# A spectral filter followed by a mixture of experts on one core: first-layer products summed in PSUM banks, a folded transform stage for three batches, six more second layers with seven products

## The chip, the cores and the metric

The program runs on one core of a Trainium2 chip. The metric is the device time of one execution in microseconds (us), as the median of several runs. Engines are named as in the profile: PE multiplies matrices and PEld loads its weights, DVE, ACT and POOL work elementwise, SP issues most of the transfers (DMA). "Bank" is one of the eight PSUM buffers of 128 x 512 float32 into which PE writes.

## The reference

Everything is float32. A filter along the sequence comes first, then a layer of experts that uses one expert for each token:

```python
# x: (8, 2496, 256), filt: (1249, 256) complex
X = np.fft.rfft(x, axis=1)
y = np.fft.irfft(X * (filt_r + 1j * filt_i)[None], n=2496, axis=1)
x = y.reshape(19968, 256)
# w_gate (256, 8), w1 (8, 256, 1024), w2 (8, 1024, 256)
logits = x @ w_gate
expert_idx = np.argmax(logits, axis=1)
gate_w = softmax(logits)[np.arange(N), expert_idx]
for e in range(8):                       # the tokens of expert e
    h = np.maximum(x_sorted[lo:hi] @ w1[e], 0.0)
    y_sorted[lo:hi] = h @ w2[e]
out = gate_w[:, None] * y_sorted[inv_perm]
```

## The kernel before

**The transform.** The length 2496 is 39 x 64, so the filter is four stages of matrix products, with a filter multiplication between the second and the third:

- A (`stage_a`, table `ta`, 39 points) reads `fin` loaded from x and stores to `zd`.
- B (`stage_b`, table `tb`, 64 points) reads `zd` back, and DVE multiplies its result with the filter `ht` into `ys`.
- C (`stage_c`, table `tc`, 64 points back) takes `ys` and stores to `ud`.
- D (`stage_d`, table `td`, 39 points back) reads `ud` back and leaves the tokens in `yo`.

So each batch goes through DRAM twice inside the transform. A and D have a plain and a folded form. The folded form uses that cosines are even and sines odd in the point number: the rows of x are summed and subtracted in pairs first (`fold_x`, two DVE operations), and four products of 64 x 64 tables in the four quarters of PE then replace two products of 117 x 120. `BA = 8, BD = 3` say from which batch on A and D are folded: A never (there are eight batches, 0 to 7), D from batch 3. Where the form changes, a table is loaded again into the same buffer (`load_table(..., 1)`).

**The experts.** `route` picks the expert of each token, POOL scatters the tokens to `rowsd` in DRAM by expert, and `tile_map` cuts the rows into tiles of 512, 256 or 128 rows of one expert. A tile of 512 rows is a first layer (`xT` times `w1`, result `hT`) and a second layer (`hT` times `w2`). With the eight batches there are 28 tiles of 512 rows here, five of them in the last batch.

- The first layer of such a tile is done in two halves, each by `hidden_by_quarters`: seven products of quarters, with sums of quarters of x (`sums`, `xT`) and of w1 (`wsum`, `w1t`), instead of eight. Each product is written to a bank of its own; DVE and ACT combine them in `hT`.
- The second layer is `result(i, j)`, four times, of 16 matmul records each, or for "wide" tiles `result_by_quarters`, also with seven products of quarters. Wide tiles need the space that the transform's buffers leave, so they start only when the transform is over (`late` is set), and end with the last tile of 512 rows. Nine tiles are wide.

**The order of the work.** PE, ACT, DVE and POOL each take their instructions in the order in which the kernel issues them. A planner, the class `Order`, keeps an estimated clock for each engine while the program is written, from a price for each kind of instruction (`count`), transfer (`transfer`, `LOAD`) and handover between engines (`HOP`). The transform's steps stand in a list, each with a due time within its batch (`slot`, the numbers called `at`); the loop at the end takes the first open step whose inputs are estimated to be there, or a product of the experts. `credit` and `share()` set how many products go between the steps. `when` says when a product can start, `side` when POOL's scatters are issued, `bank` gives the bank that is estimated to come free first. `ps.live["bank"]` lists banks that may not be given away.

Of the kernel before, what the change touches and what calls it, by code (L numbers as in the profile page):

```python
# [10 lines left out]
F32 = mybir.dt.float32  # L11
# [9 lines left out]
P = 128  # L21
# [17 lines left out]
BA, BD = 8, 3  # L39
# [134 lines left out]
class Order:  # L174


    HOP = 0.1
    LOAD = 2.0
# [42 lines left out]
    def transfer(self, out, in_):  # L221
# [3 lines left out]
        return size / n * packet / 14e3 * (1.7 if n >= 1024 and (in_ if out.space == DRAM else out).ap[0][1] <= 64 else 1.0)  # L225

    def count(self, engine, op, args, named):
# [17 lines left out]
        if out is not None:  # L245
            start = max(start, self.ahead.pop(out.name, 0.0))
            n = int(np.prod([d[1] for d in out.ap][1:])) if out.space != DRAM else 0
        tail = 0.0
        if op.endswith("dma_start"):
            busy = 1.03 if engine == "gpsimd" else 0.4  # L250
# [3 lines left out]
            took = self.transfer(out, named["in_"])  # L254
# [4 lines left out]
        else:  # L259
            if out is None:  # L260
                took = 0.8 if engine == "sync" else 0.02
            elif engine == "tensor":
# [6 lines left out]
                if op == "matmul" and rows == 64 and n > D // 2:  # L269
                    took = 0.29 if n > D else 0.17  # L270
                took *= 2.0 if start < self.slow else 1.0
                tail = 0.25
# [73 lines left out]
def kernel(  # L346
# [104 lines left out]
    ps.live["bank"] = lambda: {p.name for key, p in outs.items() if key[0] == "odd"}  # L451
# [97 lines left out]
    ins, outs, lgs, yts = {}, {}, {}, {}  # L549
    NIN, YB = 7, 6  # L550
# [303 lines left out]
    def route(b, c0, c1):  # L854
# [105 lines left out]
        if t0 + w == NG:  # L960
            rows_at[b] = nc.last + 3.0
# [30 lines left out]
    def tile_map(b, rows, n, last):  # L992
# [31 lines left out]
        erow = pools["moe"].tile([1, n], I32, tag=f"erow{n}", name="erow", bufs=2)  # L1024
# [5 lines left out]
        rrow = pools["moe"].tile([1, n], I32, tag=f"rrow{n}", name="rrow", bufs=2)  # L1030
# [108 lines left out]
    def hidden_by_quarters(h):  # L1139
# [46 lines left out]
        yield 0.85  # L1186

# [148 lines left out]
    def slot(k):  # L1336
# [12 lines left out]
        for name, of, when, at, where in (("ta", ta, BA - 2, 0.65, "a"), ("tb", tb, BA - 1, 0.76, "b"),  # L1349
                                          ("tc", tcm, BD - 1, 0.95, "c"), ("td", td, BD, 0.95, "d")):  # L1350
# [6 lines left out]
        if 0 < k < B:  # L1357
            for f in range(0, NF + 4, 2):
                at = f / (NF + 4)
                if f < NF:  # L1360
                    steps.append((at, lambda f=f: stage_b(k, f), ("z", k, f // 4) if f % 4 == 0 else None, 0.85, "b", lambda f=f: count("y") < 4 and [tables["tb"], ins["z", k, f // 4]]))
                if f >= 4:
                    steps.append((at + 0.01, lambda f=f: stage_c(k, f - 4), None, 0.85, "c", lambda f=f: [tables["tc"], outs["y", k, f - 4], 0.0 if f % 4 else sb.free("st") - 0.9]))
        if k + 1 < B:
            for c in range(nch):
                at = (0.25 if k == 0 else 0.0) + 0.7 * c / nch
# [5 lines left out]
        if k > 0:  # L1372
            for c in range(nch + 3):
                at = 0.8 * c / (nch + 3) - 0.1 if k == 1 else (0.35 if k == 2 else 0.2) + 0.8 * c / (nch + 3)
                if c < nch and k == 1:
                    steps.append((at - 0.05, lambda c=c: turn_u(c), None, 0.22 * CH[c][1], "d", lambda: ("c", 0) in stored and [zu["u"]]))
                if c < nch:
                    steps.append((at, lambda c=c: stage_d(k - 1, c), ("u", k - 1, c) if k > 1 else "y", (0.29 if k > BD else 0.43) * CH[c][1], "d",
                                  lambda c=c: count("odd") < 2 and [tables["td"], ins["u", k - 1, c] if k > 1 else outs["ui", c], sb.free("y") - 0.9]))
# [330 lines left out]
```

## Time and profile before

| | |
|---|---|
| median of 3 runs | 1455.43 us (1455.31 to 1456.91) |
| the profiled execution | 1458.61 us, its span 1456.9 us |
| PE busy in the span | 1414.6 us, 97% |
| DVE / ACT / POOL busy | 870.2 / 456.5 / 805.9 us (60 / 31 / 55%) |
| granted TensorE clock | 0.994 of full speed |

The span is the time from the first to the last instruction; 1.7 us of the profiled execution lie around it. In the rows below, `x32` counts records: a float32 matmul leaves two records, so "16 records" are eight matmul instructions. Matmul records overlap, so what one group of matmuls costs is read from the start of one group to the start of the next, not from a row's length. A row of the timeline has the start, the length, the engine, the operation with what it writes and reads, the count, and in brackets the idle time before it and what ended that.

### The profile page before, as it was taken

To read this page: it belongs to the slowest core of one execution; us is meant where nothing else is said; L and a number is where in the kernel's file an instruction comes from. 1 tells how busy PE (TensorE), PEld (TensorE's weight loads), DVE (VectorE), ACT (ScalarE), POOL (GpSimd) and SP (SyncE) were. 2 spreads that over 40 slices of the span, in tenths; PEclk is the share of its full clock that TensorE was granted. 3 is DMA by queue.
4 is the path that set the end of the run, shared out by engine and by line. 5 is a ranking of instruction groups with operands and counts; after the bars stand their busy time and mean duration, and the time that the engine had idled before them with its cause. 6 is when DMAs were issued, how large, how long until landed. Compare 5 with 4: busy or idle time off the path is not lost. (4 is left out here: it accounts for less than half of the span.)

```text
span 1456.9 us, 25907 instructions
## 1 busy us (share of the span) xinstructions
PE 1414.6 (97%) x7900; PEld 1122.0 (77%) x7900; DVE 870.2 (60%) x1880; ACT 456.5 (31%) x973; POOL 805.9 (55%) x1213
## 2 busy tenths in 40 slices
PE   8998898899999999999999999999999999999998
PEld 6543555677667767777777788889999999999997
DVE  5666649455786675577777765557778775531110
ACT  4543443333332233222222232222232322223332
POOL 3334344535746653646566676738989878831111
PEclk9998999999999999999999999999999999999999
DMA  9669698987977577558446645539654425456661
GB/s 330 228 204 314 234 295 226 309 255 227 312 206 228 146 246 193 146 154 259 146 118 164 220 118 158 153 116 252 185 172 155 130 67 144 134 193 175 175 188 48
DMA packets 216589, 281.22 MB, mean 193 GB/s; under 512 B 123228, under 2 KB 162784, under 8 KB 216450
## 3 DMA queue, kind: packets, MB, share of 16 engines
q1 hardware_dynamic: 198930, 235.20, 54.6%
q0 software_dynamic: 17520, 44.34, 8.6%
q8 instruction: 66, 1.08, 0.3%
q14 instruction: 73, 0.60, 0.1%
HBM read 197.85 MB, written 82.27 MB: 192 GB/s over the span
## 5 line engine op out<-in xcount | busy, mean ns | idle before, releaser
L298 PE MATMUL bank<-w2t,hT 128*128 128x256 f32 (+1 forms) x1984 | 390.0, 351 | 3.2 <-DMA w2t<-in_moe_w_dram 1.9
L298 DVE TENSOR_TENSOR hT<-bank,hT 128x512 f32<-128x512 f32 (+1 forms) x504 | 300.5, 626 | 147.0 <-PE bank L298 78.5
L298 PEld LDWEIGHTS bank<-w2t,hT 128*128 128x128 f32 x1984 | 335.4, 191 | 53.1 <-issue 9.3
L298 POOL DMA_INDIRECT out_dram<-ys,ng x161 | 162.0, 1006 | 285.8 <-ACT ys L298 106.3
L298 PE MATMUL bank<-xT,w1t 128*128 128x256 f32 (+1 forms) x1728 | 317.1, 329 | 2.7 <-DMA w1t<-in_moe_w_dram 2.7
L298 PEld LDWEIGHTS bank<-xT,w1t 128*128 128x128 f32 x1728 | 265.4, 192 | 37.4 <-issue 12.5
L298 ACT ACTIVATE hT<-hT 128x1024 f32<-128x1024 f32 (+1 forms) x144 | 134.5, 958 | 396.4 <-DVE hT L298 395.9
L298 POOL DMA_INDIRECT rows<-yo,row x176 | 178.8, 1016 | 70.9 <-POOL yo L298 51.6
L298 PE MATMUL bank<-sums,wsum 128*128 128x256 f32 (+1 forms) x576 | 136.5, 359 | 2.6 <-ACT ys L298 2.3
L298 ACT ACTIVATE ys<-bank,ng 128x256 f32<-128x256 f32 x95 | 45.0, 474 | 284.0 <-PE bank L298 245.0
L298 PE MATMUL bank<-w2s,hT 128*128 x592 | 132.6, 379 | 0.0
L298 PEld LDWEIGHTS bank<-w2s,hT 128*128 128x128 f32 x592 | 110.3, 190 | 13.9
L298 PEld LDWEIGHTS bank<-sums,wsum 128*128 128x128 f32 x576 | 99.7, 190 | 23.8 <-issue 6.8
L298 POOL TENSOR_TENSOR wsum<-w1t 128x256 f32<-128x256 f32 x72 | 58.5, 812 | 92.1 <-PE bank L298 71.5
L298 DVE STREAM_TRANSPOSE xT<-xg 128x512 f32<-128x512 f32 (+2 forms) x126 | 57.5, 494 | 56.2 <-PE bank L298 51.7
L298 PE MATMUL bank<-ys,tc 128*128 128x512 f32 x140 | 74.0, 616 | 6.0 <-DVE ys L298 4.2
L298 PE MATMUL bank<-fin,tb 128*128 128x512 f32 x140 | 72.3, 607 | 5.0 <-DMA fin<-zd 3.7
L298 ACT ACTIVATE hT<-bank 128x128 f32<-128x128 f32 (+1 forms) x193 | 58.2, 304 | 59.8 <-PE bank L298 57.3
L298 PE MATMUL bank<-fin,ta 117*120 117x512 f32 x154 | 74.1, 600 | 2.0 <-DMA fin<-in_x_dram 1.8
L298 DVE TENSOR_TENSOR ys<-bank,ht 128x512 f32<-128x512 f32 x80 | 54.9, 686 | 34.5 <-PE bank L298 33.9
L298 PE MATMUL bank<-xT,wsum 128*128 128x256 f32 (+1 forms) x288 | 68.3, 359 | 0.2 <-ACT lg L298 0.2
L298 PE MATMUL bank<-sums,w1t 128*128 128x256 f32 (+1 forms) x288 | 67.2, 356 | 0.0
(172 smaller groups left out, 1724.0 us busy)
## 6 DMA issues: line engine op xcount, KB each, us to landing
w1t<-in_moe_w_dram SPq DMA_DIRECT2D x126, 512.0 KB
w2t<-in_moe_w_dram SPq DMA_DIRECT2D x68, 512.0 KB
fin<-in_x_dram SPq DMA_DIRECT2D x39, 512.0 KB
fin<-zd SPq DMA_DIRECT2D x35, 512.0 KB
fin<-ud SPq DMA_DIRECT2D x35, 512.0 KB
zd<-zo SPq DMA_DIRECT2D x35, 480.0 KB
xg<-rows SPq DMA_DIRECT2D x112, 128.0 KB
ud<-uo SPq DMA_DIRECT2D x25, 504.0 KB
```

What stands on the lines that cost most here:

```text
L298: return real(*args, **named)
```

## The change

Four things change; the first three change the work itself, the fourth its order.

1. **Folded A for the last three batches.** `BA` goes from 8 to 5. Batches 5, 6 and 7 get `fold_x` and the folded `stage_a`, and the tables `ta` and `tb` loaded again in the run are now used. The built program has 33 matmuls of 120x512 fewer, and 60 of 64x512 and 12 of 64x256 more, on DVE 36 fold operations more; the loads of `zd` for these batches are two transfers each (15 transfers more on SP).
2. **Sums in banks.** For the tiles of 512 rows that aren't of the last batch (23 tiles, 46 halves) `hidden_in_banks` takes the place of `hidden_by_quarters`. The seven products stay, but four of them are added up by PE in one bank (`x`) and two in another (`y`); between these ACT copies what stands in the bank so far. The built program has 184 DVE additions of 128x512 fewer, 92 ACT copies of 128x512 more, and 46 ACT operations of 128x1024 replaced by 92 of 128x512. A half may begin its first two products before the half ahead of it has ended (`can_begin`).
3. **More wide tiles.** `share()` is at most 2.99 instead of 4.0, may fall to -0.50 instead of 0.3, and holds back 82 us of products instead of 60. In the built program 15 tiles are wide instead of nine: 192 matmuls of 128x256 fewer, 336 of 128x128 more (and 66 DVE, 24 POOL operations more).
4. **The planner's numbers.** Prices, due times, limits and slack are new throughout.

```diff
-BA, BD = 8, 3
+BA, BD = 5, 3
...
-    HOP = 0.1
-    LOAD = 2.0
+    HOP = 0.038942
+    LOAD = 3.042
...
-            busy = 1.03 if engine == "gpsimd" else 0.4
+            busy = 1.03 if engine == "gpsimd" else 0.61737
...
-    ps.live["bank"] = lambda: {p.name for key, p in outs.items() if key[0] == "odd"}
+    ps.live["bank"] = lambda: {p.name for key, p in outs.items() if key[0] == "odd"} | set(kept)
...
+    def hidden_in_banks(h):
...
+        def product(q, left, right, first=True):
+            for v in range(2):
+                mm(q[:, v], lhsT=left[:, v * P:(v + 1) * P], rhs=right, start=first and v == 0, stop=v == 1, skip_group_check=True)
...
+        first, upper, lower, last = hT[:, 0, :, 0], hT[:, 0, :, 1], hT[:, 1, :, 0], hT[:, 1, :, 1]
+        x_name, x = new_bank(True)
+        product(x, w[:, 0, 0], b[:, 0, 0])
+        nc.scalar.copy(out=first, in_=x)
+        chain[h] = 1, nc.last + nc.HOP
+        z = new_bank(False)[1]
+        product(z, w[:, 1, 0], b[:, 1, 0])
+        add(first, z, first)
+        yield
+
+        product(x, ws[:, 1], ts[:, 1], False)
+        nc.scalar.copy(out=lower, in_=x)
+        chain[h] = 0, nc.last + nc.HOP
+        y_name, y = new_bank(True)
+        product(y, w[:, 0, 1], b[:, 0, 1])
+        yield
+
+        product(x, ws[:, 0], ts[:, 0], False)
+        nc.scalar.copy(out=last, in_=x)
+        after = nc.last + nc.HOP
+        add(last, y, last)
+        chain[h] = 0, max(after, nc.last + nc.HOP - 0.85)
+        relu(first, first)
+        yield
+
+        product(x, ws[:, 2], b[:, 1, 1], False)
+        relu(upper, x)
+        product(y, w[:, 1, 1], ts[:, 2], False)
+        add(lower, y, lower)
+        both = hT[:, 1].rearrange("p v r c -> p v (r c)")
+        relu(both, both)
...
-        for name, of, when, at, where in (("ta", ta, BA - 2, 0.65, "a"), ("tb", tb, BA - 1, 0.76, "b"),
-                                          ("tc", tcm, BD - 1, 0.95, "c"), ("td", td, BD, 0.95, "d")):
+        for name, of, when, at, where in (("ta", ta, BA - 2, 1.5, "a"), ("tb", tb, BA - 1, 1.5, "b"),
+                                          ("tc", tcm, BD - 1, 1.5, "c"), ("td", td, BD, 1.5, "d")):
...
-        while sides and not (held[0] == "pool" and t["gpsimd"] > t["tensor"] + 1.5):
+        while sides and not (held[0] == "pool" and t["gpsimd"] > t["tensor"] + 0.3):
...
-        return min(4.0, max(0.3, (known - RESERVE) / max(left_t[0], 1.0)))
+        return min(2.9871, max(-0.50287, (known - 82.073) / max(left_t[0], 1.0)))
```

**Where it shows, 1: PE, one half of a first layer in the stretch of the wide tiles.** Before, the row with `w2t` is the last product of a wide second layer, and the seven rows behind it are the seven products of a half, each with a new bank number.

```order
L298 MATMUL bank_10909<-w2t_10459,hT_10687 128x128 x8
L298 MATMUL bank_10943<-xT_10516,w1t_10611 128x256 x2
L298 MATMUL bank_10947<-xT_10516,w1t_10611 128x256 x2
L298 MATMUL bank_10971<-sums_10519,wsum_10750 128x256 x2
L298 MATMUL bank_10975<-xT_10516,w1t_10611 128x256 x2
L298 MATMUL bank_10979<-sums_10519,wsum_10750 128x256 x2
L298 MATMUL bank_10984<-sums_10519,w1t_10611 128x256 x2
L298 MATMUL bank_10989<-xT_10516,wsum_10750 128x256 x2
```

Of the changed kernel, PE at the same kind of place:

```order
L300 MATMUL bank_8625<-w2t_8318,hT_8417 128x128 x8
L300 MATMUL bank_8659<-xT_8207,w1t_8385 128x256 x2
L300 MATMUL bank_8663<-xT_8207,w1t_8385 128x256 x2
L300 MATMUL bank_8659<-sums_8210,wsum_8482 128x256 x2
L300 MATMUL bank_8690<-xT_8207,w1t_8385 128x256 x2
L300 MATMUL bank_8659<-sums_8210,wsum_8482 128x256 x2
L300 MATMUL bank_8700<-xT_8508,w1t_8480 128x256 x2
L300 MATMUL bank_8704<-xT_8508,w1t_8480 128x256 x2
L300 MATMUL bank_8659<-xT_8207,wsum_8482 128x256 x2
L300 MATMUL bank_8690<-sums_8210,w1t_8385 128x256 x2
```

Bank 8659 is written four times, and before each time after the first PE waits for ACT's copy of it. Between the first two times, and between the second and the third, stands one other product; ahead of the fourth stand two, of the next half (bank 8700 and 8704).

**Where it shows, 2: ACT at the same place.** Before, the four scaled results (`ys`) of the wide tile stand ahead of the copy of the new half's first product; behind it come the two `hT<-hT` operations.

```order
L298 ACTIVATE ys_10905<-low_10760,ng_9769 128x256
L298 ACTIVATE ys_10907<-low_10760,ng_9769 128x256
L298 ACTIVATE ys_10919<-top_10759,ng_9769 128x256
L298 ACTIVATE ys_10921<-top_10759,ng_9769 128x256
L298 COPY hT_10942<-bank_10943 128x2x256
L298 ACTIVATE hT_10942<-hT_10942 128x1024 x2
```

Of the changed kernel, ACT:

```order
L300 ACTIVATE ys_8620<-low_8492,ng_7371 128x256
L300 ACTIVATE ys_8622<-low_8492,ng_7371 128x256
L300 ACTIVATE ys_8635<-top_8491,ng_7371 128x256
L300 ACTIVATE ys_8637<-top_8491,ng_7371 128x256
L300 COPY hT_8658<-bank_8659 128x2x256 x3
L300 ACTIVATE hT_8658<-hT_8658 128x2x256
L300 COPY hT_8699<-bank_8700 128x2x256
```

The four `ys` stand ahead of the first copy as before, but the three copies of bank 8659 are now ones for which PE waits. This neighbourhood, `ys` from `top` and then copies from one bank, occurs nine times.

**Where it shows, 3: SP, where the table for folded A is loaded again.** The table goes into the buffer of the old one, ahead of the loads that follow it.

```order
L300 DMA ud<-uo 42x3x1024
L300 DMA ud<-uo 2x1024
L300 DMA ta<-in_ta_dram 128x128
L300 DMA td<-in_td_dram 128x128
L300 DMA fin<-ud 128x4x256
L300 DMA fin<-in_x_dram 128x1024
L300 DMA fin<-zd 128x1024
```

In the order of issue no product on PE stands between this `ta` and the first folded A, which reads it. Before, the nearest such place was the table `tc`, with two matmuls of 128x256 between its issue and the first C product that reads it:

```order
L298 DMA w1t<-in_moe_w_dram 128x1024
L298 TENSOR_LOAD erow
L298 ISA x3
L298 DMA w2t<-in_moe_w_dram 128x1024
L298 DMA tc<-in_tc_dram 128x128
L298 DMA ud<-uo 128x1024
```

In the changed kernel some 25 matmuls stand between the issue of `tc` and its first reader, and five in the case of `tb`. Early in the program another distance shrinks: between the last C product of batch 1 and its first D product stood 18 matmuls of 512 columns, and now stand 12.

More of the change, by code (lines that the diff above doesn't have):

```diff
@@ L224, in transfer @@
         size = 4 * int(np.prod([d[1] for d in in_.ap]))
-        return size / n * packet / 14e3 * (1.7 if n >= 1024 and (in_ if out.space == DRAM else out).ap[0][1] <= 64 else 1.0)
+        return size / n * packet / 14.674 / 1e3 * (1.5686 if n >= 1024 and (in_ if out.space == DRAM else out).ap[0][1] <= 64 else 1.0)
     def count(self, engine, op, args, named):
@@ L246, in count @@
             start = max(start, self.ahead.pop(out.name, 0.0))
+            if engine == "tensor" and out.name in self.used:
+                start = max(start, self.used[out.name] + self.HOP)
             n = int(np.prod([d[1] for d in out.ap][1:])) if out.space != DRAM else 0
@@ L253, in count @@
             self.t[engine] = start + busy
-            took = self.transfer(out, named["in_"])
+            took = self.transfer(out, named["in_"]) * (1.5281 if engine == "gpsimd" else 1.0)
             self.t["transfers"] = max(self.t["transfers"], start + busy) + took
@@ L960, in route @@
         if t0 + w == NG:
-            rows_at[b] = nc.last + 3.0
+            rows_at[b] = nc.last + 3.525
     def pad_rows():
@@ L1517, in when @@
             return max(ps.free("bank"), nc.ready(w1t[n], xts[i]))
+        if n in chain:
+            banks, after = chain[n]
+            return max(ps.free("bank") - (0.85 if banks == 1 else 0.0) if banks else 0.0, ps.free("bank", 1) - 0.85 if banks == 2 else 0.0, after)
         return max(ps.free("bank"), ps.free("bank", 1) - 0.85, nc.ready(wsum[n], sums[i], xts[i]))
-    halves, ends = [0], [0]
+    halves, ends, chain = [0], [0], {}
     def first_products():
@@ L1530, in turned, with in_banks, can_begin @@
                 used["x"] += 1
+        begun = {}
+        def in_banks(i):
+            return quarters(i) and TILES[i][0] == 4 and TILES[i][1] < B - 1
+        def can_begin(h):
+            i = h // 2
+            if i >= NT - RARE or not in_banks(i) or i not in xts or h not in wsum or h % 2 and ends[0] < i:
+                return False
+            asked.add(("quarters", h))
+            return when(("quarters", h)) <= t["tensor"] + 0.3
         def half(h):
@@ L1662 @@
             more_loads()
-            for _ in range(4):
+            for _ in range(5):
                 side()
```

75 lines of the change are left out of this document (54 added, 21 removed).

## The prediction

> **What bounds the kernel now.** I read the page's head first, then the busy times by stretch, then who PE waited for, and last the timeline where a term of the sum comes from. The page says that PE is the engine that sets the time:
>
> ```profile
> span 1456.9 us, 25907 instructions
> PE 1414.6 (97%) x7900; PEld 1122.0 (77%) x7900; DVE 870.2 (60%) x1880; ACT 456.5 (31%) x973; POOL 805.9 (55%) x1213
> ```
>
> By stretch (columns: busy time and records of PE, PEld, DVE, ACT, POOL, then granted clock, DMA share, GB/s):
>
> ```profile
> 100.00:150.00 50.00, 40.73 (x120) 17.77 (x119) 33.56 (x87) 19.61 (x42) 19.29 (x31) 0.90 0.94 310
> 150.00:200.00 50.00, 45.54 (x188) 27.91 (x187) 25.47 (x61) 20.59 (x49) 21.29 (x37) 0.97 0.79 261
> 200.00:250.00 50.00, 42.60 (x184) 22.51 (x183) 37.99 (x111) 20.09 (x47) 22.00 (x35) 1.00 0.85 237
> 250.00:300.00 50.00, 46.21 (x219) 36.29 (x218) 22.68 (x62) 13.91 (x34) 30.44 (x53) 0.97 0.93 287
> 300.00:500.00 200.00, 198.93 (x1049) 142.86 (x1042) 136.08 (x305) 61.32 (x137) 110.61 (x180) 1.00 0.75 229
> 500.00:900.00 400.00, 396.53 (x2096) 304.33 (x2095) 276.71 (x587) 112.11 (x214) 235.07 (x377) 1.00 0.60 177
> 900.00:1451.00 551.00, 550.55 (x3585) 512.27 (x3583) 278.66 (x556) 159.92 (x350) 329.72 (x444) 1.00 0.53 154
> ```
>
> From 300 us on PE idles 1.07 + 3.47 + 0.45 = 5.0 us in 1151. Between 100 and 300 us it idles 24.9 us, with the DMA at 0.79 to 0.94 of its share and a clock below 1: there transfers set the time. Who PE waited for says the same (total, times, longest):
>
> ```profile
> PE bank L298 <- DMA fin<-ud: 6.5, 2, 4.6
> PE bank L298 <- DMA fin<-in_x_dram: 5.5, 4, 1.9
> ...
> PE bank L298 <- DMA w1t<-in_moe_w_dram: 2.7, 1, 2.7
> PE bank L298 <- ACT ys L298: 2.3, 1, 2.3
> PE bank L298 <- DMA w2t<-in_moe_w_dram: 1.9, 1, 1.9
> PE bank L298 <- DMA tc<-in_tc_dram: 1.8, 1, 1.8
> ...
> PE bank L298 <- DVE hT L298: 0.8, 2, 0.5
> PE bank L298 <- ACT hT L298: 0.6, 2, 0.4
> PE bank L298 <- POOL w2t L298: 0.5, 1, 0.5
> ```
>
> So work taken off PE comes off the time wherever PE has no wait, and an operation taken off DVE, ACT or POOL is worth only the few waits that name it.
>
> **Folded A.** Starts of successive groups give the prices:
>
> ```profile
> 213.41 1.02 PE L298 MATMUL bank<-fin,ta 117*120 117x512 f32 x2
> 214.28 1.02 PE L298 MATMUL bank<-ys,tc 128*128 128x512 f32 x2
> ...
> 344.37 0.66 PE L298 MATMUL bank<-fin,td 60*64 60x256 f32 x8
> 344.96 1.99 PE L298 MATMUL bank<-xT,w1t 128*128 128x256 f32 x8
> ...
> 709.89 1.09 PE L298 MATMUL bank<-fin,td 60*64 60x512 f32 x8
> 710.91 1.35 PE L298 MATMUL bank<-w2t,hT 128*128 128x256 f32 x5
> ```
>
> A plain A product costs 214.28 - 213.41 = 0.87 us, a batch 11 x 0.87 = 9.6. Folded A isn't in this trace, but folded D has the same shape: four products of 64 x 64 tables take 1.02 us with 512 columns and 0.59 with 256, a batch 5 x 1.02 + 0.59 = 5.7. Three batches: 3 x 3.88 = **-11.6 us**. By busy time in place of starts the two forms are these:
>
> ```profile
> L298 PE MATMUL bank<-fin,ta 117*120 117x512 f32 x154 | 74.1, 600 | 2.0 <-DMA fin<-in_x_dram 1.8
> L298 PE MATMUL bank<-fin,td 60*64 60x512 f32 x200 | 27.5, 613 | 2.2 <-DMA fin<-ud 1.8 <-PE bank L298 0.4
> ```
>
> 74.1 / 7 = 10.6 plain; 27.5 / 25 = 1.10 a folded group, so 6.1 a batch: 3 x 4.5 = -13.5; the folded price of this row against the plain one by starts gives 3 x 3.5 = -10.5. These are the ends. The 36 folds of 124x512 lie on DVE, the 15 more issues on SP; these batches come after 300 us, where PE's whole idle time is the 5.0 us above, so there both are covered.
>
> **Six more wide tiles.** A plain second layer of 512 rows is four groups of 16 records, a wide one seven groups of 16 shorter ones:
>
> ```profile
> 350.38 3.62 PE L298 MATMUL bank<-w2t,hT 128*128 128x256 f32 x16
> 353.93 0.26 PE L298 MATMUL bank<-rx,sel 128*32 128x16 f32 x8
> ...
> 1049.43 1.95 PE L298 MATMUL bank<-w2t,hT 128*128 128x128 f32 x16
> 1051.22 1.95 PE L298 MATMUL bank<-tsum,hsum 128*128 128x128 f32 x16
> ...
> 1314.64 3.62 PE L298 MATMUL bank<-w2s,hT 128*128 x16
> 1318.10 3.73 PE L298 MATMUL bank<-xT,w1t 128*128 128x128 f32 x32
> ```
>
> Plain: 4 x 3.55 (between steps of the transform) or 4 x 3.46 (after it) = 14.2 or 13.8; wide: 7 x 1.79 = 12.5. That is 1.3 to 1.7 us a tile; the middle, 1.4, times six is **-8.4 us** (-7.9 to -10). The DVE and POOL work of wide tiles is covered: PE waited 0.5 us in all for `w2t` from POOL and had 0.45 us idle after 900 us, and a tile brings the same load in both kernels. If POOL fell behind there, PE would wait for `tsum`.
>
> **Sums in banks.** PE does the same seven products, so nothing comes off PE itself. Off DVE come 184 additions, 0.684 us each by this row, so 126 us; 66 operations of the six wide tiles and 36 folds take at that price some 70 back. ACT gets 92 copies at 0.576 us, 53 us more.
>
> ```profile
> L298 DVE TENSOR_TENSOR hT<-bank,hT 128x512 f32<-128x512 f32 x392 | 257.4, 684 | 109.5 <-PE bank L298 74.6 <-ACT hT L298 23.3 <-DVE hT L298 0.5
> L298 ACT COPY hT<-bank 128x512 f32<-128x512 f32 x56 | 32.3, 576 | 9.1 <-PE bank L298 9.1
> ```
>
> None of this is on PE's path except where PE waited for a bank to be emptied: the 2.3, 0.8 and 0.6 us in the rows above. I take **-2 us** of these 3.7; the ends are all of them, and +2 because the transform is packed more densely.
>
> What is new is a wait: PE adds to a bank only when ACT has copied it, and all of PE's work queues behind it. The trace shows the place already, since the nine wide tiles of before end with the same ACT order:
>
> ```profile
> 1056.58 1.89 PE L298 MATMUL bank<-xT,w1t 128*128 128x256 f32 x8
> ...
> 1057.29 0.91 ACT L298 ACTIVATE ys<-top,ng 128x256 f32<-128x256 f32 x2 [0.88 <-ACT ys L298]
> 1058.10 0.56 ACT L298 COPY hT<-bank 128x512 f32<-128x512 f32 x1
> 1058.31 1.03 PE L298 MATMUL bank<-sums,wsum 128*128 128x256 f32 x4
> ```
>
> The product at 1058.31 goes to a new bank and needn't wait. In the changed kernel it goes to the bank that the copy reads until 1058.66, so PE stops 0.35 us, plus the handover, 0.4. Nine such places: 3.7 us. Elsewhere the copy starts on a free ACT: product end to copy end is 0.56 us and two short handovers, and the one product between takes 0.86, so PE has just enough; of 138 places 36 have that one product, one has none (0.8 us), the others two or more. Sum **+4.5 us**; ends 0 (ACT free in time everywhere) and +12 (each of the 36 also 0.2).
>
> **Tables and early transfers.** `ta` was loaded again before, but nobody read it; now folded A does, with nothing between issue and reader. The nearest row is the wait for `tc`, 1.8 us. Waits of this size cost more than themselves. After 1.92 us, 32 records took 298.59 - 289.93 = 8.66 us where two groups of 16 take 2 x 3.55:
>
> ```profile
> 289.93 8.83 PE L298 MATMUL bank<-w2t,hT 128*128 128x256 f32 x32 [1.92 <-DMA w2t<-in_moe_w_dram]
> 298.59 1.03 PE L298 MATMUL bank<-xT,w1t 128*128 128x256 f32 x4
> ```
>
> That is 1.56 lost to the clock. So `ta` +3.3 (1.8 + 1.5), `tc`, whose reader is now far behind, -1.8: **+1.5 us**. [...]
>
> Two more things move the early waits, in opposite directions. Batch 1's first D, which waited 4.6 us for `ud`, comes six matmuls earlier (6 x 0.87 = +5.2 if the transfer lands when it did). Against that, the planner now expects a transfer to land 1.04 us later than it did, so it should place fewer readers too early. I take these as cancelling; ends +5.2 and -11 (rival 1).
>
> **Sum:** -11.6 - 8.4 - 2 + 4.5 + 1.5 = -16.0 us. The profiled execution took 1458.61 us for a span of 1456.9, 3.2 above the median of 1455.43; the waits are a fraction of a per cent in either, so I subtract from the median: 1439.4, forecast **1439**.
>
> **Rivals.**
>
> 1. *The early DMA waits go away.* The planner has other work at hand from 160 us on, and with later landing times puts it in front: the waits for `w1t`, `tc`, `w2t`, one of the four of `in_x` (2.7 + 1.8 + 1.9 + 1.4 = 7.8) go, and two times 1.56 of half clock. For: each is a reader placed too early. Against: the DMA is at 0.79 to 0.94 there, so a moved wait comes back. -11 in place of +1.5: 1427. Chance 0.21.
> 2. *Early transfers get worse.* `ta` waits as long as `ud` did (4.6, and 1.6 of half clock) and batch 1's D takes its full +5.2; with -1.8 for `tc` that is +9.6 in place of +1.5: 1448. For: the same queue at a share of 0.9. Against: `ta` is small and the planner sees it. Chance 0.12.
> 3. *Slower: PE waits for ACT in every half.* ACT works in order, and a copy behind an `hT` operation of 1024 columns, itself waiting for DVE, comes a microsecond late. The other terms give -20.5; spread over 138 places, 0.15 us each eats that. At 0.18 (25 us) the time is 1460. For: nine places are certain. Against: only 37 of 138 have less than two products between. Chance 0.08.
> 4. *Short stops keep the clock down.* If PE's stops of 0.4 us, once a wide tile, drop the clock as the 1.92 us did, nine times 1.56 come on top: 1453, about no change. The waits of half a microsecond in the rows above (DVE and ACT `hT`, POOL `w2t`) lie after 300 us, where the clock reads 1.00; that speaks against it. Chance 0.03. [...]
>
> **How the numbers follow.** The forecast holds 0.56, with its own range 1431 to 1447: the ends of the terms, not all on one side. The range must take in most of rivals 1 and 2: **1423 to 1452**, which leaves out rivals 3 and 4 and the tails of rival 1. A difference of 0.2%, 2.9 us, is about what can be told from none. Faster than 1452.5 are the forecast, 1 and 2, 0.56 + 0.21 + 0.12 = 0.89; within 0.2%, 0.04, is rival 4 and the fast end of 3; slower 0.07.
>
> **What would show it.** PE busy falls by some 20 us. Folded A: groups `fin,ta` of 64-row form, eight records from start to start near 1.0 us. Wide tiles: `tsum,hsum` 480 records instead of 288. Sums in banks: a new wait of PE for ACT `hT`, about 0.4 us nine times at the ends of wide tiles, and DVE near 815 us busy. Tables: a PE wait for `ta` and none for `tc`. I'd be wrong first in the early stretch: if PE's idle time between 100 and 300 us moves by more than 5 us, that term failed, and if PE waits for ACT by more than 10 us in all, the sums in banks did.

## The result and the profile after

The changed kernel takes **1428.99 us** (median of four runs, 1428.35 to 1434.73), the kernel before beside it 1455.37 (1453.54 to 1456.91): ratio 0.9828, 95% interval 0.98 to 0.9856, 26.4 us faster. The same kernel in another set of runs took 1435.75 us against 1455.69, ratio 0.9865 (0.9841 to 0.9889), 19.9 us faster. The forecast was 1439, 16.4 below the median before.

The profiled execution took 1428.35 us for a span of 1426.6. The head of its page (busy time, share of the span, instructions):

```profile
span 1426.6 us, 26583 instructions
PE 1397.9 (98%) x8266; PEld 1116.4 (78%) x8266; DVE 816.6 (57%) x1749; ACT 533.6 (37%) x1167; POOL 845.8 (59%) x1231
```

PE's busy time fell by 1414.6 - 1397.9 = 16.7 us, while the span fell by 30.3: the rest, 13.6 us, is time in which PE stood still before (3.2 us of the 30.3 are the profiled execution of before, which was that far above its median). Busy times by stretch say where (columns as before: PE, PEld, DVE, ACT, POOL, granted clock, DMA share, GB/s):

```profile
100.00:150.00 50.00, 44.42 (x163) 21.09 (x162) 36.80 (x94) 22.58 (x48) 23.73 (x38) 0.93 0.93 313
150.00:200.00 50.00, 49.44 (x197) 28.81 (x196) 34.19 (x103) 24.59 (x54) 27.75 (x47) 1.00 0.95 339
200.00:250.00 50.00, 45.59 (x207) 29.17 (x206) 38.32 (x86) 21.56 (x50) 25.67 (x42) 0.93 0.89 262
250.00:300.00 50.00, 50.00 (x295) 34.85 (x294) 37.70 (x98) 16.68 (x47) 27.71 (x49) 1.00 0.89 304
300.00:500.00 200.00, 196.77 (x1081) 135.97 (x1080) 145.53 (x306) 72.99 (x165) 115.82 (x176) 0.99 0.86 260
500.00:900.00 400.00, 396.26 (x2323) 322.14 (x2322) 230.10 (x519) 148.08 (x300) 274.64 (x408) 1.00 0.60 177
900.00:1421.00 521.00, 518.21 (x3528) 484.58 (x3526) 229.54 (x417) 177.25 (x402) 310.27 (x411) 1.00 0.50 140
```

From 100 to 300 us PE idles 5.58 + 0.56 + 4.41 + 0.00 = 10.55 us instead of 24.92, and puts 862 records there where 711 stood. The DMA is a little fuller than before: over the whole stretch its share is 0.92 at 304 GB/s, before 0.88 at 274. From 300 us on it idles 3.23 + 3.74 + 2.79 = 9.8 us instead of 5.0. The list of what PE waited for (total, times, longest) is a different one:

```profile
PE bank L300 <- ACT hT L300: 8.2, 14, 2.8
PE bank L300 <- DMA fin<-zd: 4.2, 1, 4.2
PE bank L300 <- POOL sums L300: 3.9, 1, 3.9
...
PE bank L300 <- DVE av L300: 1.4, 1, 1.4
PE bank L300 <- DVE hT L300: 1.4, 1, 1.4
...
PE bank L300 <- DMA w1t<-in_moe_w_dram: 0.5, 1, 0.5
```

The waits for `ud`, `in_x`, `w2t` and `tc` are gone and the one for `w1t` is 0.5 instead of 2.7 us (in the second profile of this kernel `in_x` is there with 1.9, at 8.7 us, and `ud` with 0.5); DVE's `ys` (4.2 in four waits before) is gone and ACT's `ls` is 0.6 instead of 2.7; `zd` is one wait of 4.2 where it was two of 3.7 together; the one for POOL's `sums` is new; and ACT's `hT` has gone from 0.6 to 8.2. Between 100 and 300 us the waits for transfers fell from 17.95 to 4.7 us, those for other engines from 6.9 to 5.9. The groups that the prediction priced (busy us, mean ns of one, idle before them), `fin,ta` by its two forms, the products of wide tiles, and the additions and copies of the sums:

```profile
L300 PE MATMUL bank<-fin,ta 117*120 117x512 f32 x88 | 41.8, 593 | 0.0
...
L300 PE MATMUL bank<-fin,ta 60*64 60x512 f32 x120 | 16.3, 615 | 0.0
...
L300 PE MATMUL bank<-tsum,hsum 128*128 128x128 f32 x480 | 58.5, 275 | 0.0
...
L300 DVE TENSOR_TENSOR hT<-bank,hT 128x512 f32<-128x512 f32 x208 | 140.3, 685 | 167.9 <-ACT hT L300 96.8 <-PE bank L300 68.6
...
L300 ACT COPY hT<-bank 128x512 f32<-128x512 f32 x148 | 86.1, 582 | 104.7 <-PE bank L300 104.7
```

### The profile page after: what moved, and what is told of

Same layout as the page of the kernel before. It is cut to its first block, busy times and chain, and to the rows that moved or that the text cites. A ratio compares the mean times of both kernels' runs of the same rounds, so it can differ in the third digit from the quotient of the medians.

```text
span 1426.6 us, 26583 instructions
## 1 busy us (share of the span) xinstructions
PE 1397.9 (98%) x8266; PEld 1116.4 (78%) x8266; DVE 816.6 (57%) x1749; ACT 533.6 (37%) x1167; POOL 845.8 (59%) x1231
## 3 DMA queue, kind: packets, MB, share of 16 engines
q8 instruction: 69, 1.13, 0.3%
## 5 line engine op out<-in xcount | busy, mean ns | idle before, releaser
L300 PE MATMUL bank<-w2t,hT 128*128 128x256 f32 (+1 forms) x1984 | 349.6, 330 | 0.3 <-ACT hT L300 0.3
L300 PEld LDWEIGHTS bank<-w2t,hT 128*128 128x128 f32 x1984 | 308.1, 191 | 41.2 <-issue 10.9
L300 DVE TENSOR_TENSOR hT<-bank,hT 128x512 f32<-128x512 f32 (+1 forms) x320 | 184.0, 593 | 217.1 <-ACT hT L300 125.6
L300 ACT ACTIVATE hT<-hT 128x512 f32<-128x512 f32 (+1 forms) x144 | 117.1, 825 | 187.5 <-DVE hT L300 187.5
L300 PE MATMUL bank<-sums,wsum 128*128 128x256 f32 (+1 forms) x576 | 141.6, 369 | 11.1 <-ACT hT L300 7.2
L300 ACT COPY hT<-bank 128x512 f32<-128x512 f32 (+1 forms) x164 | 91.9, 560 | 104.9 <-PE bank L300 104.7
L300 ACT ACTIVATE hT<-bank 128x128 f32<-128x128 f32 (+2 forms) x259 | 90.9, 353 | 94.1 <-PE bank L300 90.0
L300 PEld LDWEIGHTS bank<-w2s,hT 128*128 128x128 f32 x592 | 109.8, 190 | 13.5
L300 POOL TENSOR_TENSOR wsum<-w1t 128x256 f32<-128x256 f32 x72 | 54.8, 760 | 42.0 <-PE bank L300 41.5
```

The source lines that it names most:

```text
L300: return real(*args, **named)
```

## The experiments

Besides PE's idle time, the expectations below use a second measure, **lost time**: every PE record's time to the next record's start, less the median of its form, added up over a stretch. It is worked out from all rows of the timeline and holds what idle time leaves out, the half clock after a wait (in the changed kernel 1.7 us behind the one that ended at 429.62) and the small handovers from one form to another. The middle column is the least certain: by medians taken over other groups of the same rows it moves by 1 to 4 us a run, and before and changed then differ there by 2.5 to 4 us instead of 7.6, so it should be read with the idle time beside it. Every order of the plan gives another number of wide tiles, at about 1.4 us each; the comparisons below say where that matters.

| run | ratio to before, 95% | wide tiles | PE idle 100 to 300 | lost 100 to 300 | lost 300 to 780 | lost after 780 |
|---|---|---|---|---|---|---|
| before | 1 | 9 | 24.9 | 37.8 | 15.5 | 4.8 |
| changed | 0.9828 (0.98 to 0.9856) | 15 | 10.5 | 19.8 | 23.1 | 9.7 |
| changed, again | 0.9865 (0.9841 to 0.9889) | 15 | 12.5 | 23.6 | 24.9 | 10.2 |
| products apart | 0.9864 (0.9819 to 0.9909) | 12 | 14.3 | 26.4 | 26.6 | 1.4 |
| plain first stage | 0.9963 (0.994 to 0.9987) | 14 | 12.2 | 20.4 | 32.1 | 10.7 |
| old transfer prices | 0.9896 (0.9866 to 0.9926) | 14 | 14.2 | 27.0 | 30.3 | 10.0 |
| old due times | 0.9913 (0.9887 to 0.9938) | 13 | 10.7 | 19.8 | 24.0 | 15.0 |
| results on DVE | 0.9836 (0.981 to 0.9861) | 15 | 10.7 | 20.2 | 28.2 | 6.3 |
| order alone | 0.996 (0.9941 to 0.9978) | 12 | 13.4 | 20.6 | 27.9 | 4.2 |
| old choice | 0.9946 (0.9925 to 0.9968) | 14 | 15.4 | 26.2 | 32.8 | 9.7 |
| gates and results on DVE | 0.9806 (0.978 to 0.9832) | 14 | 13.0 | 22.3 | 27.3 | 6.1 |
| old share | 0.9878 (0.9849 to 0.9907) | 10 | 11.1 | 18.5 | 26.0 | 13.2 |
| old prices and choice | 0.9821 (0.9792 to 0.9849) | 14 | 18.5 | 29.8 | 20.3 | 9.6 |
| before, new prices and choice | 1.0002 (0.9982 to 1.0022) | 9 | 21.1 | 33.1 | 24.7 | 8.1 |

Two numbers say how far a row may be read: the changed kernel against before gave 0.9828 in one set of runs and 0.9865 in another, and its own lost time differed by 6 us between the two profiles, 3.8 of them from 100 to 300 us. Between runs of different sets (1 to 4; 5 to 7 with the changed kernel again; 8 to 11) differences under 0.4% are not told from none.

**1. The products apart again.** Every half of a first layer is done as before, all else stays:

```diff
         def in_banks(i):
-            return quarters(i) and TILES[i][0] == 4 and TILES[i][1] < B - 1
+            return False
```

> The changed kernel with hidden_by_quarters in every tile: each product in a bank of its own again, and so no waits of PE for ACT between products of one bank. The planner then makes 12 wide tiles instead of 15 (three times 1.4 us more on PE). Theory S (the sums in banks only cost PE time: some 13 us of waits for ACT hT and DVE hT in the changed kernel, and what they take off DVE hides nothing): about 1429 - 13 + 4 = 1420, PE waits for ACT hT near zero. Rival R (the additions that they take off DVE pay: without them DVE empties banks late in the denser transform): PE waits for banks behind DVE instead, 1430 to 1440.

Measured: 1438.42 us, ratio 0.9864, with three wide tiles fewer (4.2 us). The lost time after 780 us falls from 9.7 to 1.4, since the stops for ACT are gone; instead DVE, which has its additions back, is late in the transform:

```profile
PE bank L300 <- DVE hT L300: 5.7, 3, 2.8
...
PE bank L300 <- ACT hT L300: 1.3, 1, 1.3
```

Less the 4.2 us of the tiles, that is between 0.1% worse and 0.3% better than the two results of the changed kernel: the sums in banks by themselves are worth nothing that the runs can tell, a wait for one engine against a wait for another. The early stretch loses 26.4 us in this run, though neither prices nor choice nor due times were touched: 6 to 7 us is what another order can move there by itself (run 6, with neither the sums nor the fold, loses 20.6).

**2. First stage plain.**

```diff
-BA, BD = 5, 3
+BA, BD = 8, 3
```

> The changed kernel with BA = 8: plain A in all batches, planner numbers as changed, 14 wide tiles. By the forecast's price folded A is worth 11.6 us, and one wide tile 1.4: 1429 + 13 = 1442, with PE idle between 100 and 300 us as in the changed kernel (10 us). Rival: the folded stage shortens the early waits too, then 1450 and more idle time of PE before 300 us.

Measured: 1454.33 us, ratio 0.9963, so 14 to 20 us above the changed kernel, of which 1.4 is a wide tile. The time is the rival's and the early idle time, 12.2 us, the forecast's. Not all of it is the fold's own work: from 300 to 780 us PE idles 9.96 us here, 4.35 in the changed kernel, and the granted clock reads 0.50 in two stretches of 6.83 us (from 308.51 and 564.51 us) instead of one of 3.41. The span is 27.7 us longer than the changed kernel's; idle time and half clock (half of PE's busy time at 0.50) take 12.9 of it, the tile 1.4, and 13.4 are left for the fold; against the second profile of the changed kernel it is 20.3 - 6.5 - 1.4 = 12.4. The early stretch stays good without it.

**3. The old prices of transfers** in the planner:

```diff
-    LOAD = 3.042
+    LOAD = 2.0
...
-            busy = 1.03 if engine == "gpsimd" else 0.61737
+            busy = 1.03 if engine == "gpsimd" else 0.4
-            took = self.transfer(out, named["in_"]) * (1.5281 if engine == "gpsimd" else 1.0)
+            took = self.transfer(out, named["in_"])
```

(with them, the rate 14.674 and the factor 1.5686 in `transfer` go back to 14 and 1.7.)

> The changed kernel with the planner's four old prices of transfers (LOAD 2.0, 14 and 1.7 in transfer, 0.4 for an issue on SP, POOL's scatters without the factor 1.53); 14 wide tiles (1.4 us more on PE). Theory P (the early waits shrank because the planner now expects transfers to land later): the 15 us that PE's idle time between 100 and 300 us fell come back, 1440 to 1448, with PE waiting for fin and w1t by DMA again. Rival D (the due times did it): 1428 to 1433, idle time there still near 10 us.

**4. The old due times** of the transform's steps and of the tables (all the numbers `at`, among them these):

```diff
-        for name, of, when, at, where in (("ta", ta, BA - 2, 1.5, "a"), ("tb", tb, BA - 1, 1.5, "b"),
+        for name, of, when, at, where in (("ta", ta, BA - 2, 0.65, "a"), ("tb", tb, BA - 1, 0.76, "b"),
...
-                at = -0.10494 + 1.3496 * f / (NF + 4)
+                at = f / (NF + 4)
```

> The changed kernel with the old due times of all steps (the numbers called at, and the places of the table loads); prices, limits and share as changed; 13 wide tiles (2.8 us more on PE). Theory D (due times): PE's idle time between 100 and 300 us returns toward 25 us, 1440 to 1448. Rival P (transfer prices): 1430 to 1434, idle time near 10 us.

Measured: 0.9896 and 0.9913. The early stretch loses 27.0 us with the old prices, 7 of the 18 that the change had saved, and 19.8 with the old due times, none of them. So the due times did not make the early stretch better. The 7 is no more than run 1 lost without touching the prices, so it isn't shown to be theirs; the time of run 3, 1445.41 us, lies where theory P put it, but not by the mechanism that it named. Run 4 is slower than its rival had it, by the ratios 7 to 12 us above the changed kernel; 2.8 us of that are two wide tiles, and the lost time after 780 us is 15.0 instead of 9.7.

**5. The changed kernel again, and the results of the wide tiles on DVE.** In half of the results of a wide tile, those from `top`, the scaling moves from ACT to DVE, so that ACT has the copies free at the tile's end:

```diff
-            nc.scalar.activation(ys, y.rearrange("p n d -> p (n d)"), AF.Copy, scale=gate[:, j])
+            if j < 2:
+                nc.vector.tensor_scalar(ys, in0=y.rearrange("p n d -> p (n d)"), scalar1=gate[:, j], scalar2=None, op0=ALU.mult)
+            else:
+                nc.scalar.activation(ys, y.rearrange("p n d -> p (n d)"), AF.Copy, scale=gate[:, j])
```

> The changed kernel once more, beside the next runs on the same chip, as their measure: 0.982 of before, as it was.

> The changed kernel with one edit: the two scaled results from top at the end of a wide tile are made by DVE instead of ACT, so that ACT is free for the copy of the next half's first product. The planner's order hardly moves (15 wide tiles as before the edit). Theory S (PE's wait of 0.5 us at nine ends of wide tiles is ACT's queue): these waits go to at most 0.1 us, and 9 x 0.45 = 4 us with them, 0.997 of the changed kernel. Rival: DVE is the later one there (it has its own additions behind), and the waits stay or pass to DVE hT, no change in time.

Measured in one set: 1435.75 and 1432.18 us, 3.6 less. One of the nine places in the profile of the changed kernel (start, length, engine, what, idle before and what ended it):

```profile
823.10 1.89 PE L300 MATMUL bank<-xT,w1t 128*128 128x256 f32 x8
...
823.81 0.91 ACT L300 ACTIVATE ys<-top,ng 128x256 f32<-128x256 f32 x2 [0.88 <-ACT ys L300]
...
824.62 0.56 ACT L300 COPY hT<-bank 128x512 f32<-128x512 f32 x1
...
825.33 0.89 PE L300 MATMUL bank<-sums,wsum 128*128 128x256 f32 x3 [0.34 <-ACT hT L300]
```

The two `ys` hold ACT until 824.62, the copy ends at 825.18, and PE goes on at 825.33. PE's list of waits has 14 for ACT's `hT` in the changed kernel, and with the scaling on DVE six, and from 780 to 1400 us PE is 3.04 us busier; the first row is the second run of the changed kernel, the second the edit:

```profile
780.00:1400.00 620.00, 614.64 (x4123) 571.78 (x4122) 298.64 (x557) 214.31 (x447) 396.45 (x517) 1.00 0.54 154
```

```profile
780.00:1400.00 620.00, 617.68 (x4153) 575.44 (x4152) 309.36 (x587) 204.28 (x423) 397.64 (x519) 1.00 0.55 155
```

So the nine stops are shown, and their cause is the pair of `ys` ahead of the copy. By the profile they are 9 x 0.34 = 3.06 us of idle time; the 3.6 us between the medians agrees, but holds other moves too (3.4 us less lost time early, 3.3 more from 300 to 780 us), and the two intervals overlap. The stop of 0.77 us at the end of the last of these tiles is still there with the edit.

**6. The order alone.** Both work changes that the planner doesn't make by itself are undone:

```diff
-BA, BD = 5, 3
+BA, BD = 8, 3
...
         def in_banks(i):
-            return quarters(i) and TILES[i][0] == 4 and TILES[i][1] < B - 1
+            return False
```

> The changed kernel with BA = 8 and hidden_by_quarters in every tile: the work of before, but for 12 wide tiles instead of nine (4.2 us less on PE), in the new order. Theory O (the early gain is the new order's alone): PE's lost time between 100 and 300 us is near 20 to 25 us instead of 38, and the time 0.989 of before. Rival W (it comes with the changed work: folds and fewer additions make DVE empty banks earlier): lost time near 38 us, 0.997 of before.

Measured: ratio 0.996, 5.8 us faster than before in its set, of which three more wide tiles are 4.2. The early stretch is as good as in the changed kernel, first row before, second this run:

```profile
100.00:300.00 200.00, 175.08 (x707) 104.47 (x705) 119.70 (x318) 74.19 (x171) 93.03 (x154) 0.96 0.88 274
```

```profile
100.00:300.00 200.00, 186.63 (x797) 108.25 (x796) 144.83 (x376) 82.83 (x186) 98.33 (x165) 0.98 0.91 298
```

So the early gain needs neither the fold nor the sums in banks; it is the order's. But 300 to 780 us loses 27.9 us where before lost 15.5 (idle 8.59 and 4.54, and half clock in two places where before had none), and what is left of the order by itself is 5.8 - 4.2 = 1.6 us, within what can't be told from none: theory O had the early stretch right and the time, 0.989, not. This run and run 1 differ by the fold alone, with twelve wide tiles in both: 0.996 - 0.9864 = 0.0096, 14.0 us, though across two sets (the two intervals together are about 7 us either way).

**7. The old choice among ready steps.**

```diff
-            for f in fs[:28]:
+            for f in fs[:16]:
...
-            pick, late_by = next((c for c in choice if c[1] <= 0.05), min(choice, key=lambda c: c[1]) if choice else (None, 0.5))
-            if late_by > 0.05:
-                t["tensor"] += min(late_by, 1.061)
+            pick, late_by = next((c for c in choice if c[1] <= 0.2), min(choice, key=lambda c: c[1]) if choice else (None, 0.5))
+            if late_by > 0.2:
+                t["tensor"] += min(late_by, 0.5)
```

> The changed kernel with the old way of choosing the next step: 16 steps in view instead of 28, a step taken when it is at most 0.2 us late instead of 0.05, the clock moved on by at most 0.5 instead of 1.06; 14 wide tiles. Theory C (the stricter choice is what shortened the early waits, since neither old transfer prices nor old due times brought them back whole): lost time of PE between 100 and 300 us back at 30 us or more, 0.992 of before. Rival: no one of the planner's numbers does it alone, lost time again 20 to 27 us, 0.985 to 0.991.

Measured: ratio 0.9946, slower than both the theory and its rival had it, with 26.2 us lost early: some 6 of the 18, but only 2.6 more than the changed kernel lost in the same set, and as much as run 1. Runs 8 to 11 ask what is behind the early and the middle stretch.

**8. The copy of the gates on DVE too.** The longest single wait of PE for ACT stands in the transform, not at a wide tile. In the changed kernel:

```profile
424.83 1.13 PE L300 MATMUL bank<-sums,wsum 128*128 128x256 f32 x4
...
425.79 1.03 PE L300 MATMUL bank<-xT,w1t 128*128 128x256 f32 x4
...
428.66 0.16 DVE L300 SCALAR_TENSOR_TENSOR row<-lids,bank 128x8 uint32<-128x8 f32 x1
428.91 0.17 ACT L300 COPY gts<-bank 128x8 f32<-128x8 f32 x1 [4.44 <-DVE row L300]
428.97 0.59 ACT L300 COPY hT<-bank 128x512 f32<-128x512 f32 x1
...
429.62 1.84 PE L300 MATMUL bank<-sums,wsum 128*128 128x256 f32 x4 [2.79 <-ACT hT L300]
...
431.25 2.90 PE L300 MATMUL bank<-xT,w1t 128*128 128x256 f32 x8
```

The product that the copy at 428.97 reads, the first row, ended at 425.96, and ACT was idle. But ACT's queue had a small copy of the routing, `gts`, ahead, which waited 4.44 us for DVE's `row`, and behind it stood the copy for which PE waits. After the wait PE ran at half clock (the granted clock reads 0.50 from 429.88 to 433.30): four records took 431.25 - 429.62 = 1.63 us where 0.86 is usual, and more than half of the next eight were as slow, 1.7 us in all by the clock. The edit, on top of that of run 5 (14 wide tiles):

```diff
-            nc.scalar.copy(out=sd.rearrange("p (c g) -> p g c", g=4), in_=pr[:, :, 1])
+            nc.vector.tensor_copy(sd.rearrange("p (c g) -> p g c", g=4), pr[:, :, 1])
```

> Changed kernel with two edits: the results ys of the top experts are scaled on DVE instead of ACT, as in the run with results on DVE, and the copy gts<-bank in the routing goes from ACT to DVE. Fourteen wide tiles instead of fifteen, which costs 1.4 us. Theory (a copy hT<-bank stands behind an ACT instruction that waits for DVE's row): the PE waits of 2.8 and 1.0 us at the two routings, and some 1.6 us of half clock behind the longer one, go; 4 us less than the run with results on DVE, 1.4 back: about 0.985 x 1 of that run's ratio, that is 2.5 us below it, a ratio to the kernel before near 0.982. Rival (DVE itself is late there, whoever waits): the waits come back under DVE's name, and the run is 1 to 2 us above the run with results on DVE.

Measured: 1436.28 us against 1461.7, ratio 0.9806 (0.978 to 0.9832). PE's waits for ACT's `hT` are down to one of 0.4 us, so the reading of the queue holds (the 0.77 us at the end of the last wide tile are still there, listed under another name). But waits of other names are there instead:

```profile
PE bank L300 <- ACT ls L300: 4.5, 3, 2.8
...
PE bank L300 <- DVE hT L300: 1.9, 3, 0.9
...
PE bank L300 <- DVE ls L300: 1.6, 2, 1.4
...
PE bank L300 <- ACT hT L300: 0.4, 1, 0.4
```

The lost time from 300 to 780 us is 27.3 us, 28.2 in run 5, and the idle time 8.80 and 8.57: the rival's reading, since the edit moved the waits to the next thing that is late there. The ratio is the one that the theory gave, and the lowest of all, but its interval overlaps those of the changed kernel and of run 5, so it isn't shown to be faster than either.

**9. The old rule for spreading the transform.**

```diff
-        return min(2.9871, max(-0.50287, (known - 82.073) / max(left_t[0], 1.0)))
+        return min(4.0, max(0.3, (known - RESERVE) / max(left_t[0], 1.0)))
```

> Changed kernel with the old rule for how the transform is spread over the layers (the share of known work, 0.3 to 4 with the old reserve, in place of -0.5 to 2.99). Ten wide tiles instead of fifteen: +7 us of PE work. Theory (the stretch from 300 to 780 us loses 23 us instead of 15 because the transform is packed more densely there): the lost time of that stretch falls to 15 to 18, and the time is 7 - 6 = about 1 us above the changed kernel. Rival (it is lost to the sums in banks and the orders of ACT and DVE, however dense): the lost time stays at 22 to 25 and the time is 7 us above the changed kernel.

Measured: ratio 0.9878, 26.0 us lost from 300 to 780: the rival's. By idle time the stretch is even worse, first row the changed kernel, second this run:

```profile
300.00:780.00 480.00, 475.65 (x2650) 351.11 (x2649) 309.66 (x690) 176.34 (x388) 305.88 (x480) 1.00 0.70 210
```

```profile
300.00:780.00 480.00, 467.90 (x2519) 338.12 (x2518) 305.87 (x634) 173.44 (x367) 260.81 (x414) 0.99 0.69 199
```

So spreading the transform by the old rule doesn't take the loss away. (The time, 0.9878, lies 7 us above one result of the changed kernel and 2 above the other, and tells nothing between the two.)

**10 and 11. Old prices and old choice together, and the new ones in the kernel before.** The edits of runs 3 and 7 in one; and the reverse of both, in the old kernel.

> Changed kernel with both the old prices of transfers and the old choice among ready steps (16 looked at, 0.2 us of lateness let pass, 0.5 at most). Fourteen wide tiles, +1.4 us. Each of the two alone brought back about 7 of the 18 us that 100 to 300 us lost less than before. Theory (the two together are what made the early stretch better): lost time there 33 us or more, time 13 to 18 us above the changed kernel. Rival (either edit only reorders, and part of the gain comes from the rest of the order): lost time at most 28, time 8 to 12 us above.

> Kernel before with the new prices of transfers and the new choice among ready steps, nothing else: products, folds and due times are the old ones, nine wide tiles. Theory (prices and choice make the early stretch better by themselves): lost time from 100 to 300 us falls from 38 to about 25, and the time is 10 to 13 us below the kernel before (ratio 0.991 to 0.993). Rival (they do it only with the new due times, shares or sums in banks): lost time stays at 34 or more, ratio 0.997 to 1.003.

The early stretch in the two, run 10 first:

```profile
100.00:300.00 200.00, 181.55 (x812) 103.62 (x811) 143.34 (x374) 81.96 (x187) 99.33 (x162) 0.95 0.91 293
```

```profile
100.00:300.00 200.00, 178.91 (x712) 108.97 (x711) 125.12 (x345) 77.97 (x176) 94.93 (x161) 0.96 0.87 275
```

Of the 14.4 us of idle time saved, taking both back returns 18.45 - 10.54 = 7.9, and putting both into the old kernel saves 24.92 - 21.09 = 3.8. Neither theory is right in full. Against the 14.3 us that PE idles in run 1, which has the new prices and the new choice, the 18.5 of run 10 is 4 more, so prices and choice are at most a part of it; the rest hangs on the order as a whole. In the ratios neither is seen. Run 10 loses 10 us more early and 3 less in the middle, and its ratio is 0.9821, that of the changed kernel; run 11 loses 4.7 less early and 9.2 more in the middle, and its ratio is 1.0002 (its profiled execution was 5.4 us above its median). Runs 3 and 7, each with half of the edit of run 10, are slower than run 10. In runs 10 and 11 what one of the two stretches gained the other lost; in runs 3 and 7 both were worse.

## Why the prediction was right

**The sum.** The forecast was -16, measured -26.4 in one set of runs and -19.9 in another. Both lie in the range of 1423 to 1452; 1428.99 is 2 us below the likeliest one's own range, and nearer to rival 1 (1427) than to 1439. The two terms for PE's own work were right. That the sum came out in the range is in part luck: the early stretch gave back 14 us of idle time for which the sum had +1.5 of loss, and losses after 300 us that it hadn't either took some of that away.

**Folded A: right, somewhat low.** A folded group takes 232.92 - 231.90 = 1.02 us, as the sum had it from folded D:

```profile
231.90 1.09 PE L300 MATMUL bank<-fin,ta 60*64 60x512 f32 x8
232.92 1.12 PE L300 MATMUL bank<-fin,tb 128*128 128x512 f32 x2
```

Over all folded and plain groups, start to start, 69.7 us before and 15.0 + 1.8 + 39.0 = 55.8 after: -13.9, just past the far end of -10.5 to -13.5, since some plain groups before ran at half clock (four records at 122.68 us are 2.63 us long, 1.88 elsewhere). The time moved by 14 (run 6 against run 1) to 13 to 18 (run 2, less its tile; 12.4 to 13.4 when its extra waits and half clock are taken off). The cover held: no wait for `fold_x` or the extra SP issues appears. That these batches come after 300 us was wrong, though harmless: the first folded group starts at 231.9 us.

**Six more wide tiles: right.** 480 records of `tsum,hsum`, and at 0.216 us a record of 256 columns and 0.112 of 128 these are 384 x 0.216 - 672 x 0.112 = 7.7 us less PE work, against the 8.4 of the sum; all starts of second layers with their waits and half clock, 423.2 before and 413.0 after, give 10.2. POOL kept up: no wait for `tsum`. (PE busy fell by 16.7 us where some 20 were named; the rows overlap and stretch at half clock (four records at 429.62 are 1.84 us long, 1.13 at 424.83), so starts are the better measure.)

**Sums in banks: the right mechanism, too small.** The nine stops came as drawn, each with 0.34 us idle against 0.4 (0.5 by starts: 825.33 - 823.10 = 2.23 us where eight records take 1.72), and one of 0.77 against 0.8: together 3.8 us idle, and 4.5 predicted. What the step failed to see is a third kind of place: ACT's queue holding a copy behind an instruction that waits for DVE. That gives 2.79 us and 1.7 of half clock at 429.62, and 0.96 at 511.77, where the term allowed 0.2 for a place with one product between. PE's waits for ACT's `hT` are 8.2 us in all, some 11 with this half clock and the 9 x 0.16 us by which the nine places are longer by starts (an estimate), so the cost was near the upper end of 0 to +12. The gain opposite was too small as well: without the sums in banks (run 1) DVE's `hT` costs 5.7 us of waits, and PE runs at a granted clock of 0.50 for 10.2 us between 300 and 780 us, 3.4 in the changed kernel. So -2 and +4.5 were both too small, and run 1 can't tell their difference from nothing.

**Tables and early transfers: the step that failed.** The term was +1.5, with "I take these as cancelling"; the stretch from 100 to 300 us gave 14.4 us of idle time back, 13 of them in waits for transfers. The prediction had held against rival 1 that with the DMA at 0.79 to 0.94 of its share a wait that is moved comes back; it didn't, and the transfers moved faster in that stretch (304 GB/s after 274). `ta` cost nothing: issued at 226.93, read first at 231.90, with work of others for 5 us between them. "Nothing between issue and reader" was read from the order of issue, where SP's place isn't SP's time: SP ran 5 us ahead of PE there.

```profile
226.93 0.38 SPq L300 DMA_DIRECT2D ta<-in_ta_dram  x1
```

The sign that the prediction named, idle time there moving by more than 5 us, came. The likelier case had been rival 1, and its mechanism is half right: the waits it named are gone, but that the new landing times did it isn't shown: prices and choice together return 4 to 8 of the 14.4 us by runs 10 and 11, and run 1 has 3.7 of them back without either. The cause stays open. Due times, share and fold are excluded one by one by runs 4, 9 and 2, fold and sums together by run 6; the planner's numbers for matmuls and handovers (`HOP` and the end of a matmul among them), the limits for POOL's side work and the buffers that were made larger (`erow`, `rrow`) were not tried apart, nor was any interplay of more than two.

**What the prediction had no term for:** the stretch from 300 to 780 us loses 7.6 us more than before by the table, and 4.9 more after 780. The second is mostly ACT's stops (3.8 us of idle time in ten places; another 1.35 is a wait for DVE's `hT`). Of the first, the traces show 1.5 us: PE idles 4.35 us where it idled 4.54, and one stretch of half clock costs 1.7. The rest are small losses between groups of records, and their size hangs on the medians taken; no run here singled out a cause. By idle time and half clock alone, which need no median, the account is: before 100 us -3.7, to 300 us -16.6, to 780 us +1.5, after it +5.0, together -13.8 of the 30.3 us by which the span fell. The other 16.5 are PE's work, -21.6 by the two terms above, less some 5 us of small losses that aren't explained.

**Rivals 2, 3 and 4:** no wait for `ud`; PE waits for ACT's copy in 13 places of 138 (the fourteenth wait for `hT` is that of a second layer), not in every half; and the clock stays at 1.00 over the nine stops.

## What to carry to other kernels

Work taken off the engine that sets the time was paid back for the most part and could be priced from rows of the same shape: -20.0 predicted for fold and wide tiles, -21.6 found. What a new order does to waits was not: the order by itself (run 6) gained 17 us in one stretch and gave 8 to 12 back in the next, so an order's gain has to be read over the whole span. Before an operation is given to another engine's queue, look at what stands ahead of it in that queue and what *that* waits for: an idle ACT was no help while a 0.17 us copy at its head waited 4.44 us for DVE.

## What was not expected of the hardware

**The half clock came after some waits of PE and not after others of about the same length.** The same wait at the routing, 2.79 us in the changed kernel and 2.73 in run 5, was followed by half clock at once in the one, and in the other only after six records at full speed:

```profile
433.84 1.13 PE L300 MATMUL bank<-sums,wsum 128*128 128x256 f32 x4 [2.73 <-ACT hT L300]
434.81 3.30 PE L300 MATMUL bank<-xT,w1t 128*128 128x256 f32 x8
437.90 1.35 PE L300 MATMUL bank<-xT,wsum 128*128 128x256 f32 x4
439.09 1.03 PE L300 MATMUL bank<-sums,w1t 128*128 128x256 f32 x4
```

The first four records take 434.81 - 433.84 = 0.97 us, the next eight 3.09 where 1.72 is usual, the four behind them 1.19 and the next are normal again. By single records the half clock begins at 435.14, 1.30 us after the wait, and ends at 438.55, that is 3.41 us; in the changed kernel the granted clock reads 0.50 for 3.41 us from 429.88, 0.26 us after the wait. The wait of 1.92 us in the prediction ended at 289.93, and the clock reads 0.50 for 3.41 us from 291.12. Other waits of the kernel before had no half clock behind them:

```profile
177.99 1.10 PE L298 MATMUL bank<-ys,tc 128*128 128x512 f32 x2 [1.78 <-DMA tc<-in_tc_dram]
...
231.29 0.48 PE L298 MATMUL bank<-ident,ls 128*117 128x128 f32 x2 [2.74 <-ACT ls L298]
```

The granted clock reads 1.00 from 175.07 to 291.12 us there. The same holds for the 2.00 us for `zd` that ended at 107.45 and the 2.29 for `ys` at 527.43, and in the changed kernel for the waits of 1.40 and 1.35 us (DVE's `av`, `hT`). So the length of the wait alone doesn't decide it: that waits of this size cost more than themselves, as the prediction had it, held for its row of 1.92 us and not for these, and the 1.78 us for `tc`, from which it took the price of `ta`, cost no half clock. In the two long early waits of the changed kernel, 4.18 us until 107.60 and 3.89 until 219.44, the clock fell before the wait was over, at 105.62 and 218.26, and read 0.50 for 6.83 us each:

```profile
219.44 2.08 PE L300 MATMUL bank<-sums,wsum 128*128 128x256 f32 x4 [3.89 <-POOL sums L300]
...
221.31 1.91 PE L300 MATMUL bank<-xT,w1t 128*128 128x256 f32 x4
```

Groups of four took 1.87 and 1.71 us from start to start where 0.86 is usual, until 225.08.

**The sets of runs differ.** The kernel before had medians of 1455.4, 1460.4, 1455.7 and 1461.7 us in the four sets (the last three on three different chips), and the changed kernel gained 26.4 us in the first and 19.9 in the third. Its profile there has the same list of waits, 8.1 us for ACT's `hT`, and 3.8 us more lost time early.
